# Constants as immediates, a selection matrix from POOL, and one more filter chunk turned by TensorE

## The chip, the cores and the metric

The kernel runs on one core of a Trainium2 chip. A core has five engines with queues of their own: TensorE (PE in the profile; its weight loads are PEld), VectorE (DVE), ScalarE (ACT), GpSimd (POOL) and SyncE (SP), which here issues all transfers. The metric is the device time of one execution in microseconds, as the median of several runs; lower is better.

## The reference

Two independent heads share one output, side by side in the last axis. All inputs are bfloat16, the sequence has S = 2048 rows and the width is D = 576.

```python
def _A_ref(q, k, v, shift_k, ssm_k, ssm_D):     # a gated long convolution
    k_shift = sum over t < 4 of k_pad[:, t:t + S, :] * shift_k[:, 3 - t]
    kv = k_shift * v
    y = irfft(rfft(kv, padded to 2S) * rfft(ssm_k, padded to 2S))[:, :S]
    y = y + kv * ssm_D
    return q * y

def _B_ref(x, wqkv, wo):                        # linear attention, 32 heads of 18
    q, k, v = split(x @ wqkv)
    phi = lambda t: where(t > 0, t + 1, exp(t)) + 1e-6
    num, den = phi(q) @ (phi(k).T @ v), phi(q) @ sum(phi(k))
    return (num / (den + 1e-6)) @ wo
```

## The kernel before

**Order and buffers.** The whole program is one hand-made order of units, the table `ORDER` (L32 to L58): each word names a unit, its chunk and parts, the engine that does its copies (D VectorE, A ScalarE, P POOL) and, after the slash, the buffers it takes. The engines then run their shares strictly in the order in which the table issues them, and semaphores join them. So a unit's place in the table is its place on every engine that it uses, SP's queue included. PSUM is cut into four slots, numbered 0 to 3, of 4 KB per partition (two banks each). A tile may be written into a slot only when the tile that stood there last has been read. In `u1.2.0.0.A/03` the 0 is an SBUF buffer for the result and the 3 the PSUM slot.

**Head A.** The width is cut into five chunks of 128 (the last 64). A chunk's filter row set `h_sb` (128 channels x 2048 taps) must be turned so that taps lie on partitions: `hT`, by the unit hT (L507). Three ways exist. With 'D' TensorE turns 16 pieces of 128 x 128 into one PSUM slot (L516) and VectorE copies the slot out (L311). With 'a' ScalarE first sorts the row by 16 strided runs into `hp` (L521) and a DMA transfer turns it (L525). With 'p' POOL sorts (L523) instead. Chunks 0 to 2 use 'D', chunk 3 'a', chunk 4 'p'. The buffers of `h_sb`, `hp` and `hT` are three, numbered 0 to 2. A unit hd (L501) adds the skip weight `ssm_D` to the first tap.

Then both the turned filter (h) and the product `kv` (u, made by conv on VectorE and POOL) go through a two-stage Fourier transform: `s1` multiplies with the cosine and sine matrices `G` on TensorE into `s_ps` (L537), the result is copied out as `Ch` or `Cu`, a DMA transfer turns it (`Cth`, `Ctu`, unit tr), `s2` does the second stage (L560) and is copied out as `T` or `SU`. `prod` multiplies the two spectra (L572 to L577), `i1` (L594, copied out as `V`) and `i2` (L607 to L609) go back and multiply by `q`. The chunks overlap: while chunk 1 is in its products, chunk 2 is in s1 and chunk 3's filter is turned.

The matrices `G` are made in the kernel, as Sin on ScalarE of an integer phase, with the bias minus pi (L231); a small matrix of 16 points the same way (L236). The bias is a column `negpi` in SBUF, to which the instruction points.

**Head B.** `b_k` and `b_q` multiply x with the weights; `phi` (L446) does exp(t - 1) on ScalarE with the bias column `neg1` (L448) and the rest in one VectorE instruction (L449). There are 16 of these for k, 8 for q and 2 for q's last 64 columns. `b_G` (L655) multiplies x with phi(k) into `g_ps`, 4 full products and one of 64 columns; VectorE copies one column of each to `ex` (L652), and ScalarE adds it as a bias when it copies the rest (L653). The denominators are spread over the 18 columns of a head by matmuls with a selection matrix `esel` (128 x 576): row p has ones in the 18 columns of head p mod 32 (bc and bt, L749 and L760). It is made early by unit es (L105): ScalarE copies four 32 x 32 blocks of the identity and then widens them.

**Around the fourth turn.** The table issues the inverse stage of chunk 0, whose last three units (`i1.0.0.1.A/0`, `i1.0.1.0.A/1`, `i1.0.1.1.A/3`) have ScalarE copy V out, the last of them from PSUM slot 3. Then come products of chunk 1, conv of chunk 2, two s2 copies `SU`, the second transfer of `F` (FT.1.T, `G` turned), hT.3, hd.4, G.3 (slot 1), conv of chunk 3, and `u1.2.0.0.A/03`, which is the first s1 of chunk 2's u and takes slot 3.

Of the kernel before, what the change touches and what calls it, by code (L numbers as in the profile page):

```python
# [9 lines left out]
BF = mybir.dt.bfloat16  # L10
I32 = mybir.dt.int32
I16 = mybir.dt.int16
ACT = mybir.ActivationFunctionType
ALU = mybir.AluOpType
# [6 lines left out]
TWO_PI = 2.0 * math.pi  # L21
# [20 lines left out]
h1.2.1.1.A/1 cv.2.1.DD pT.0.0.P hd.3 pS.0.0.D q.1.1/3 h2.1.0.0.A/32 h2.1.0.1.A/0 G.1/1 cv.2.2.DP h1.2.0.0.A/2 pA.0.1.N  # L42
h1.2.0.1.A/0 u2.1.1.1.D/03 zs/01 ut.1.0/1 u2.1.1.0.A/2 pA.0.0.N i1.0.0.0.D/13 i1.0.0.1.A/0 i1.0.1.0.A/1 zz/2
i1.0.1.1.A/3 pX.1.1.D/0 pA.1.1.N vl.1/0 cv.2.3.DDD ht.2.0/0 pT.1.1.D u2.1.0.1.A/10 u2.1.0.0.A/2 ht.2.1/1 FT.1.T
hT.3.a/02 hd.4 G.3/1 cv.3.0.D cv.3.1.DD u1.2.0.0.A/03 lwv pS.1.1.D u1.2.1.1.A/0 G.0/2 cv.3.2.DD u1.2.1.0.A/1 pX.1.0.D/1
pA.1.0.N u1.2.0.1.A/3 G.4/0 h2.2.1.1.A/22 cv.3.3.DDD h2.2.1.0.A/1 ut.2.0/1 G.2/3 h2.2.0.0.D/00 wom lwo i2.0.1/2
h2.2.0.1.A/1 u2.2.0.0.A/03 i2.0.0/0 h1.3.0.1.D/11 ut.2.1/0 h1.3.0.0.A/2 h1.3.1.0.A/3 kv/0 u2.2.0.1.A/2 h1.3.1.1.A/1
pT.1.0.D pS.1.0.D i1.1.1.1.A/03 hT.4.p/01 i1.1.1.0.A/0 cv.4.0.D den/2 cv.4.1.PP ht.3.1/1 u2.2.1.1.D/11 i1.1.0.1.D/3
i1.1.0.0.A/0 pX.2.0.D/0 u2.2.1.0.A/1 M.2.A/2 i2.1.0/3 i2.1.1/0 M.3.A/1 ht.3.0/0 h2.3.1.1.A/12 bc.2/31 st.0 u1.3.1.1.A/00
u1.3.0.0.A/2 bt/3 h1.4.1.0.A/10 u1.3.0.1.A/1 h2.3.1.0.D/2 pT.2.0.P u1.3.1.0.A/0 h2.3.0.1.A/33 bc.0/12 M.1.A/0 ut.3.0/1  # L50
h1.4.1.1.D/1 h1.4.0.1.A/3 h2.3.0.0.A/0 bc.3/23 pS.2.0.N h1.4.0.0.A/1 M.0.A/0 ut.3.1/0 pA.2.0.P M.4.A/1 bc.1/20
# [53 lines left out]
def _esel(tc, cpool, K):  # L105
    nc = tc.nc
    K.esel = cpool.tile([128, D], BF, name="esel")
    e32 = cpool.tile([128, 32], BF, name="e32")
    for p in range(0, 128, 32):
        nc.scalar.activation(out=e32[p:p + 32, :], in_=K.ident[p:p + 32, p:p + 32], func=ACT.Copy)  # L110
    nc.scalar.activation(out=K.esel[:].rearrange("p (h e) -> p h e", e=18),
                         in_=e32[:].unsqueeze(2).to_broadcast([128, 32, 18]), func=ACT.Copy)


def _small(tc, cpool, slot, K):
# [110 lines left out]
def _sine(tc, cpool, K, ri, h):  # L226
    b = slice(8 * h, 8 * h + 8)
    if ri not in K.G:
        K.G[ri] = cpool.tile([128, 16, 128], BF, name="G%d" % ri)
    src = K.mp[:, b] if ri else K.mc[:, 1, b]  # L230
    tc.nc.scalar.activation(out=K.G[ri][:, b], in_=src, func=ACT.Sin, scale=TWO_PI / 8192, bias=K.negpi[:])  # L231


def _sine16(tc, K):
    nc = tc.nc
    nc.scalar.activation(out=K.sm[:, 1536:1984], in_=K.wi, func=ACT.Sin, scale=TWO_PI / 16, bias=K.negpi[:])  # L236
    nc.scalar.preload_act_table_set("natural_log_exp_and_others")
    nc.scalar.activation(out=K.warm[:], in_=K.neg1[:], func=ACT.Exp)

# [14 lines left out]
def kernel(  # L254
# [13 lines left out]
    nc = tc.nc  # L268
# [18 lines left out]
    cpool = ctx.enter_context(tc.tile_pool(name="consts", bufs=1, side="left"))  # L287
# [68 lines left out]
    K = Consts()  # L356
# [88 lines left out]

    def phi(ps_ap, out_ap, n):  # L446

        nc.scalar.activation(out=out_ap, in_=ps_ap, func=ACT.Exp, bias=K.neg1[0:n, :])  # L448
        nc.vector.scalar_tensor_tensor(out=out_ap, in0=out_ap, scalar=1.0, in1=ps_ap, op0=ALU.min, op1=ALU.max)  # L449

    def b_k(r):
        ps = psum.tile([128, 1024], FP32, name="k_ps")
        rr = r % 4
        for n0, n1 in ((0, 512), (512, 576)):
            for t in range(5):
                nc.tensor.matmul(ps[:, n0:n1], lhsT=xT[r // 4][:, t, rr * 128:(rr + 1) * 128],  # L456
                                 rhs=wqk[:, t, D + n0:D + n1], start=(t == 0), stop=(t == 4))
        phi(ps[:, 0:D], pk[:, r, 0:D], 128)

    def b_q(g, half):  # L460
        ps = psum.tile([128, 2, 512], FP32, name="q_ps")
        for j in range(2):
            c = 2 * half + j
            for t in range(5):
                nc.tensor.matmul(ps[:, j, :], lhsT=wqk[:, t, 128 * c:128 * c + 128], rhs=xT[g][:, t, :],  # L465
                                 start=(t == 0), stop=(t == 4))
        phi(ps[:], pqT[:, 2 * half:2 * half + 2, g * 512:(g + 1) * 512], 128)

    def b_qt(p):
        ps = psum.tile([128, 512], FP32, name="qt_ps")  # L470
        for t in range(5):
            for i, g in enumerate(PAIR[p]):
                nc.tensor.matmul(ps[64 * i:64 * i + 64, :], lhsT=wqk[:, t, 512:576], rhs=xT[g][:, t, :],
                                 start=(t == 0), stop=(t == 4))
        phi(ps[:], pq4[:, p, :], 128)
# [350 lines left out]
    def store_A(i):  # L826
# [8 lines left out]
        'dl': load_D, 'dc': turn_D, 'id': lambda: _ident(tc, cpool, K), 'io': lambda: _small(tc, cpool, slotx, K),  # L835
        'ix': lambda p, h: _dft_index(tc, slotx, K, p, h), 'iv': lambda: _w16_phase(tc, K),
        'iw': lambda: _w16_index(tc, K), 'wk': lambda: _w16_mask(tc, K), 'sin': lambda ri, h: _sine(tc, cpool, K, ri, h),
        'sw': lambda: _sine16(tc, K), 'W': lambda: _w16(tc, cpool, K),
        'FT': f_T, 'hc': lambda: _head_consts(tc, cpool, K), 'es': lambda: _esel(tc, cpool, K), 'xd': x_D,
        'hl': h_load, 'hd': h_D, 'hT': h_T,  # L840
        'kl': lambda g: load_g('k', k, g),
# [53 lines left out]
```

## Time and profile before

| | |
|---|---|
| median of 3 runs | 157.73 us (157.4 to 157.91) |
| span of the profiled execution, first to last instruction | 156.1 us |
| median less span | 1.6 us |
| TensorE clock granted | 1.000 |
| ScalarE sort of chunk 3 (L521) | 4.04 us, from 78.62 |
| DMA queue q1, share of 16 engines' span | 90.7% |
| HBM read, written | 14.97 MB, 4.72 MB |

The page's execution has a span of 156.1 us; it lists no separate time for that execution, so the median of the runs stands beside it. Sums are made against the span and carried to the median with the difference of 1.6 us.

How to read the rows quoted below: a timeline row has start and length in microseconds, the engine, the line, the operation, output<-input with shapes, a count, and in brackets how long the engine stood idle before and what released it. A row of the chain has start, length and what. A row of groups has the count, the busy time, the mean length of one in ns, and the idle time before.

### The profile page before, as it was taken

Reading aid. Unit: us, or ns where it says so; the run is one execution under the profiler, and the core shown is the slowest. Engines: PE = TensorE matmul, PEld = TensorE weight load, DVE = VectorE, ACT = ScalarE, POOL = GpSimd, SP = SyncE. Lnnn points to the kernel's source line nnn. Section 1 sums busy time; section 2 is a strip of 40 time slices with the busy share of each in tenths; the row PEclk is TensorE's granted clock in tenths of the full one; section 3 lists DMA queues with packets and bytes.
Section 4 is the critical chain, followed back from the end, with each engine's and each line's share of the span. In section 5 each row is a group of like instructions: output and inputs, shape, how many; then the busy total and the mean of one; then the engine's idle time right before and its main releaser. Section 6 shows DMA issues by size and latency. Waiting matters only on the chain.

```text
span 156.1 us, 4608 instructions
## 1 busy us (share of the span) xinstructions
PE 148.3 (95%) x1986; PEld 90.6 (58%) x1986; DVE 134.2 (86%) x169; ACT 130.8 (84%) x162; POOL 60.3 (39%) x70
## 2 busy tenths in 40 slices
PE   7999999999999999999999999999988999999990
PEld 2686564466633456457566558767555656568650
DVE  6989769899899798997899999899999979997530
ACT  4999999989998899959999767997998978897431
POOL 6038701908310974007300019457999050230000
PEclk9999999999999999999999999999999999999999
DMA  2997999999999699999999879977779997636086
GB/s 92 380 294 188 296 300 145 252 296 281 201 178 234 135 312 235 166 231 302 178 171 199 220 134 232 144 139 136 231 156 179 149 325 187 156 117 182 0 231 197
DMA packets 74315, 31.92 MB, mean 204 GB/s; under 512 B 52090, under 2 KB 73653, under 8 KB 74294
## 3 DMA queue, kind: packets, MB, share of 16 engines
q1 hardware_dynamic: 74294, 31.62, 90.7%
q8 instruction: 15, 0.25, 0.6%
q14 instruction: 6, 0.05, 0.1%
HBM read 14.97 MB, written 4.72 MB: 126 GB/s over the span
## 4 chain that ended last, share of the span: by engine, by line
PE 62%; DMA 12%; ACT 11%; DVE 8%; issue 2%; POOLq 2%; POOL 1%; SPq 1%; DVEq 0%; ACTq 0%
PE k_ps L456 10%; PE g_ps L662 10%; PE s_ps L537 8%; PE q_ps L465 6%; DMA q<-in_A_q_dram 6%; PE i_ps L594 5%; PE s_ps L560 4%; PE o_ps L783 4%; DMA Cth<-Ch 3%; DMA Ctu<-Cu 3%; DVE q L609 2%; DVE pqT L753 2%; PE i_ps L607 2%; PE i_ps L608 2%; ACT G L231 2%
## 5 line engine op out<-in xcount | busy, mean ns | idle before, releaser
L456 PE MATMUL k_ps<-wqk,xT 128*128 128x512 bf16 (+1 forms) x160 | 21.5, 286 | 0.0
L537 PEld LDWEIGHTS <-G 128*128 128x128 bf16 x320 | 17.2, 98 | 3.1 <-issue 2.3
L465 PE MATMUL q_ps<-xT,wqk 128*128 128x512 bf16 x80 | 18.4, 380 | 0.0
L309 ACT ACTIVATE Cu<-s_ps 128x1024 bf16<-128x1024 f32 (+1 forms) x19 | 17.3, 957 | 0.4 <-PE s_ps L537 0.2
L456 PEld LDWEIGHTS <-xT 128*128 128x128 bf16 x160 | 11.4, 98 | 10.5 <-issue 0.3
L662 PE MATMUL g_ps<-pk,x_sb 128*128 128x512 bf16 (+1 forms) x128 | 16.5, 286 | 0.0
L309 ACT ACTIVATE V<-i_ps 128x1024 bf16<-128x1024 f32 x16 | 15.5, 1025 | 1.1 <-PE i_ps L594 0.8
L309 ACT ACTIVATE Ch<-s_ps 128x1024 bf16<-128x1024 f32 (+1 forms) x17 | 15.7, 952 | 0.3 <-PE s_ps L537 0.3
L309 ACT ACTIVATE T<-s_ps 128x1024 bf16<-128x1024 f32 x15 | 14.8, 1026 | 0.8 <-PE s_ps L560 0.7
L309 ACT ACTIVATE ob<-o_ps 128x576 bf16<-128x576 f32 (+1 forms) x14 | 8.8, 635 | 7.4 <-PE o_ps L775 4.2
L783 PE MATMUL o_ps<-wo_M,pqT 128*128 128x512 bf16 (+1 forms) x112 | 15.0, 287 | 0.0
L495 DVE TENSOR_TENSOR at<-at 128x2048 bf16<-128x2048 bf16 (+1 forms) x12 | 14.2, 1181 | 0.9 <-POOL at L494 0.4
L449 DVE SCALAR_TENSOR_TENSOR pk<-pk,k_ps 128x576 bf16<-128x576 bf16 x16 | 11.9, 752 | 3.4 <-ACT pk L448 3.2
L309 ACT ACTIVATE SU<-s_ps 128x1024 bf16<-128x1024 f32 x14 | 14.1, 1027 | 0.7 <-PE s_ps L560 0.6
L494 DVE TENSOR_TENSOR at<-k,Wj 128x2048 bf16<-128x2048 bf16 (+1 forms) x12 | 14.1, 1171 | 0.0
L495 POOL TENSOR_TENSOR at<-at 128x1024 bf16<-128x1024 bf16 (+1 forms) x3 | 8.3, 2772 | 14.0 <-DVE at L494 10.9
L609 DVE TENSOR_TENSOR q<-i_ps,q 128x1024 bf16<-128x1024 f32 (+1 forms) x10 | 11.0, 1114 | 3.1 <-PE i_ps L608 2.8
L662 PEld LDWEIGHTS <-x_sb 128*128 128x128 bf16 x128 | 8.4, 97 | 8.9 <-issue 1.2
L448 ACT ACTIVATE pk<-k_ps,neg 128x576 bf16<-128x576 f32 x16 | 11.6, 741 | 1.5 <-PE k_ps L456 1.0
L465 PEld LDWEIGHTS <-wqk 128*128 128x128 bf16 x80 | 7.4, 98 | 9.2 <-issue 1.5
L783 PEld LDWEIGHTS <-pqT 128*128 128x128 bf16 x112 | 7.5, 98 | 7.9 <-issue 1.2
L594 PE MATMUL i_ps<-W,T 64*128 64x128 bf16 x160 | 11.2, 217 | 0.6 <-DVE pqT L753 0.5
(163 smaller groups left out, 336.0 us busy)
## 6 DMA issues: line engine op xcount, KB each, us to landing
x_sb<-in_B_x_dram SPq DMA_DIRECT2D x4, 576.0 KB, 6.9
h_sb<-in_A_ssm_k_dram SPq DMA_DIRECT2D x4, 512.0 KB, 5.8
out_dram<-ob SPq DMA_DIRECT2D x7, 288.0 KB, 4.0
k<-in_A_k_dram SPq DMA_DIRECT2D x1, 1280.0 KB
v<-in_A_v_dram SPq DMA_DIRECT2D x1, 1280.0 KB
q<-in_A_q_dram SPq DMA_DIRECT2D x1, 1280.0 KB, 8.6
wqk<-in_B_wqkv_dram SPq DMA_DIRECT2D x2, 576.0 KB, 8.4
k<-in_A_k_dram SPq DMA_DIRECT2D x1, 1024.0 KB, 8.8
```

Source lines behind the costliest of these rows:

```text
L309: nc.scalar.activation(out=out, in_=in_, func=ACT.Copy)
L448: nc.scalar.activation(out=out_ap, in_=ps_ap, func=ACT.Exp, bias=K.neg1[0:n, :])
L449: nc.vector.scalar_tensor_tensor(out=out_ap, in0=out_ap, scalar=1.0, in1=ps_ap, op0=ALU.min, op1=ALU.max)
L456: nc.tensor.matmul(ps[:, n0:n1], lhsT=xT[r // 4][:, t, rr * 128:(rr + 1) * 128], rhs=wqk[:, t, D + n0:D + n1], start=(t == 0), stop=(t == 4))
L465: nc.tensor.matmul(ps[:, j, :], lhsT=wqk[:, t, 128 * c:128 * c + 128], rhs=xT[g][:, t, :], start=(t == 0), stop=(t == 4))
L494: on[0].tensor_tensor(out=t_, in0=kk[:, 3 - stage:19 - stage], in1=wb(stage), op=ALU.mult)
L495: on[1].tensor_tensor(out=a_, in0=a_, in1=t_, op=ALU.add)
L537: nc.tensor.matmul(ps[:, bi, 0:dc], lhsT=K.G[ri][:, b, :], rhs=xf(b), start=True, stop=True)
L594: nc.tensor.matmul(ps[:, r, g, :], lhsT=s[key, hf][64 * r:64 * r + 64, z, x, 128 * g:128 * g + 128], rhs=K.W[64 * r:64 * r + 64, m, :], st ...
L609: nc.vector.tensor_tensor(out=qs, in0=ps[:, :, 0:dc], in1=qs, op=ALU.mult)
L662: nc.tensor.matmul(ps[:, n0:n1], lhsT=x_sb[:, r, f0:f0 + fn], rhs=pk[:, r, n0:n1], start=(r == 0), stop=(r == 15))
L783: nc.tensor.matmul(pss[i][:, n0:n1], lhsT=pqT[:, c, r * 128:(r + 1) * 128], rhs=B['M'][:, c, n0:n1], start=(c == 0 and not first), stop=(c ...
```

## The change

Four edits:

1. The bias of all Sin and of phi's Exp is a number in the instruction, no longer a pointer to a column. The columns are still filled, and two tiny table-warming instructions still use them.
2. `esel` is made by POOL alone: filled with ones, then four selections, each on 32 partitions x 576, keep the ones of the own head.
3. hT.3 goes from 'a' to 'D': TensorE turns it into PSUM slot 3, VectorE copies it to buffer 0. Sort and transfer go.
4. hT.4 keeps 'p', but its sorted copy goes to buffer 2, because buffer 0 now holds chunk 3's turned filter.

```diff
-hT.3.a/02 hd.4 G.3/1 cv.3.0.D cv.3.1.DD u1.2.0.0.A/03 lwv pS.1.1.D u1.2.1.1.A/0 G.0/2 cv.3.2.DD u1.2.1.0.A/1 pX.1.0.D/1
+hT.3.D/03 hd.4 G.3/1 cv.3.0.D cv.3.1.DD u1.2.0.0.A/03 lwv pS.1.1.D u1.2.1.1.A/0 G.0/2 cv.3.2.DD u1.2.1.0.A/1 pX.1.0.D/1
...
-pT.1.0.D pS.1.0.D i1.1.1.1.A/03 hT.4.p/01 i1.1.1.0.A/0 cv.4.0.D den/2 cv.4.1.PP ht.3.1/1 u2.2.1.1.D/11 i1.1.0.1.D/3
+pT.1.0.D pS.1.0.D i1.1.1.1.A/03 hT.4.p/21 i1.1.1.0.A/0 cv.4.0.D den/2 cv.4.1.PP ht.3.1/1 u2.2.1.1.D/11 i1.1.0.1.D/3
...
     K.esel = cpool.tile([128, D], BF, name="esel")
-    e32 = cpool.tile([128, 32], BF, name="e32")
+    nc.gpsimd.memset(K.esel[:], 1.0)
     for p in range(0, 128, 32):
-        nc.scalar.activation(out=e32[p:p + 32, :], in_=K.ident[p:p + 32, p:p + 32], func=ACT.Copy)
-    nc.scalar.activation(out=K.esel[:].rearrange("p (h e) -> p h e", e=18),
-                         in_=e32[:].unsqueeze(2).to_broadcast([128, 32, 18]), func=ACT.Copy)
+        m = K.esel[p:p + 32].rearrange("p (h e) -> p h e", e=18)
+        nc.gpsimd.affine_select(out=m, in_=m, compare_op=ALU.is_equal, fill=0.0, base=0,
+                                pattern=[[-1, 32], [0, 18]], channel_multiplier=1)
...
-    tc.nc.scalar.activation(out=K.G[ri][:, b], in_=src, func=ACT.Sin, scale=TWO_PI / 8192, bias=K.negpi[:])
+    tc.nc.scalar.activation(out=K.G[ri][:, b], in_=src, func=ACT.Sin, scale=TWO_PI / 8192, bias=-math.pi)
...
-    nc.scalar.activation(out=K.sm[:, 1536:1984], in_=K.wi, func=ACT.Sin, scale=TWO_PI / 16, bias=K.negpi[:])
+    nc.scalar.activation(out=K.sm[:, 1536:1984], in_=K.wi, func=ACT.Sin, scale=TWO_PI / 16, bias=-math.pi)
...
-        nc.scalar.activation(out=out_ap, in_=ps_ap, func=ACT.Exp, bias=K.neg1[0:n, :])
+        nc.scalar.activation(out=out_ap, in_=ps_ap, func=ACT.Exp, bias=-1.0)
```

What this moves on the engines, as the difference of the two programs. On ScalarE, at the place of hT.3 (V, SU and wv_GT are the copies named above, Dcol the skip weights):

```order
 L309 ACTIVATE V<-i_ps 128x8x32x4 x3
 L309 ACTIVATE SU<-s_ps 128x2x512 x2
-L521 ACTIVATE hp<-h_sb 128x2048
 L505 ACTIVATE h_sb<-h_sb,Dcol 64x1
 L653 ACTIVATE wv_GT<-g_ps,ex 128x576
```

The sort is gone, and the skip weight of chunk 4 and the copy of G.3 follow the two SU directly.

On VectorE, at the same place (T is a product of spectra of chunk 1, ex the column of G.3, at the conv of chunk 3):

```order
 L498 TENSOR_TENSOR v<-at,v 128x16x128
 L574 TENSOR_TENSOR T<-SU,T 128x2048
+L311 COPY hT<-hT_ps 128x2048
 L652 COPY ex<-g_ps 128x1
 L492 TENSOR_TENSOR at<-k,Wj 128x2048
```

A copy of the turned chunk now stands between the product and the ex column.

On TensorE 16 pairs of a weight load and a turn, of which the first is shown, are put between the s2 stage of chunk 1 and G.3:

```order
 L560 LDWEIGHTS W_329
 L560 MATMUL s_ps<-Ctu,W_329 32x512
+L516 LDWEIGHTS h_sb
+L516 MATMUL hT_ps<-ident,h_sb 128x128
...
 L662 LDWEIGHTS x_sb
 L662 MATMUL g_ps<-pk,x_sb 128x512
```

G.3's matmuls come after the turns; everything later on TensorE keeps its order.

## The prediction

> **What bounds the kernel now.** I read the page's busy shares and its chain first, then a table of stretches, then the timeline around the changed places.
>
> ```profile
> span 156.1 us, 4608 instructions
> PE 148.3 (95%) x1986; PEld 90.6 (58%) x1986; DVE 134.2 (86%) x169; ACT 130.8 (84%) x162; POOL 60.3 (39%) x70
> PE 62%; DMA 12%; ACT 11%; DVE 8%; issue 2%; POOLq 2%; POOL 1%; SPq 1%; DVEq 0%; ACTq 0%
> 30.00:48.20 18.20, 17.80 (x171) 9.86 (x172) 17.08 (x17) 16.99 (x19) 6.11 (x5) 1.00 1.10 240
> 48.20:104.00 55.80, 55.80 (x841) 34.52 (x841) 51.31 (x65) 48.12 (x54) 21.13 (x8) 1.00 1.02 205
> 104.00:120.00 16.00, 14.37 (x210) 8.79 (x207) 15.88 (x15) 14.01 (x20) 14.18 (x6) 1.00 0.80 172
> ```
>
> The last three rows are stretches: length, then the busy time of PE, PEld, DVE, ACT and POOL with their instructions, the granted clock and the load of the DMA engines. Averages mislead here: from 48.2 to 104 us TensorE has no idle time at all, and from 104 to 120 VectorE is the full one (15.88 of 16). A busy TensorE could still be a paced one, so I look at the chain where the new work goes, and at an earlier turn of a filter chunk:
>
> ```profile
> 38.97 0.99 PE hT_ps L516 x16
> 75.75 0.56 PE s_ps L560 x16
> 76.31 4.06 PE g_ps L662 x32
> 80.37 0.91 PE s_ps L537 x16
> 81.27 3.95 PE g_ps L662 x32
> ```
>
> The pieces join without gaps: TensorE issues at its own pace there, and any microsecond put on it is paid. ScalarE is busy, but up to 104 us the page gives little sign that TensorE waits for it.
>
> **Fourth chunk turned by TensorE.** The old ScalarE sort goes, with its transfer; in their place come 16 turns and one VectorE copy.
>
> ```profile
> 74.10 2.85 ACT L309 ACTIVATE V<-i_ps 128x1024 bf16<-128x1024 f32 x3
> 76.24 3.94 PE L662 MATMUL g_ps<-pk,x_sb 128*128 128x512 bf16 x26
> 78.62 4.04 ACT L521 ACTIVATE hp<-h_sb 128x2048 bf16<-128x2048 bf16 x1
> 80.07 1.22 DVE L574 TENSOR_TENSOR T<-SU,T 128x2048 bf16<-128x2048 bf16 x1
> 80.21 1.07 PE L537 MATMUL s_ps<-v,G 128*128 128x128 bf16 x16
> 81.20 0.15 DVE L652 COPY ex<-g_ps 128x1 f32<-128x1 f32 x1
> 82.68 0.74 ACT L653 ACTIVATE wv_GT<-g_ps,ex 128x576 bf16<-128x576 f32 x1
> 85.58 0.74 ACT L653 ACTIVATE wv_GT<-g_ps,ex 128x576 bf16<-128x576 f32 x1 [0.35 <-DVE ex L652]
> 95.66 1.52 PE L537 MATMUL s_ps<-hT,G 128*128 128x128 bf16 x24
> L311 DVE COPY hT<-hT_ps 128x2048 bf16<-128x2048 bf16 x3 | 3.7, 1219 | 0.1
> L516 PE MATMUL hT_ps<-ident,h_sb 128*128 128x128 bf16 x48 | 3.5, 225 | 0.1
> hT<-hp SPq DMA_TRANSPOSE x2, 4.1
> ```
>
> What it removes: ScalarE is free of 4.04 us at 78.6. That is worth nothing by these rows: at 85.58 ScalarE already waits for VectorE, so the sort's delay was used up within 3 us, under the g_ps matmuls. The dropped transfer could start at 78.62 + 4.04 = 82.66 and takes 4.1 to land (last row), so its data lay ready at 86.8 for the matmuls at 95.66: no gain. On SP the loads queued behind it go out earlier, and what they load is read later still: 0, and no row shows a loss from it.
>
> What it adds, step by step, in the time of before. The turns write PSUM slot 3, whose last tile is that of the third V eviction, which ends at 74.10 + 2.85 = 76.95. TensorE is at this point at 76.24, so it now waits 0.71 us. Sixteen turns take 0.99: 77.94. The g_ps product (4.06) ends at 82.00. Next on TensorE stands s_ps<-v,G for u1.2.0.0, again in slot 3, so it must wait for VectorE's copy of the turns. VectorE is in order and full: it finishes T at 81.20 (where the next instruction starts today) and copies until 81.20 + 1.22 = 82.42. So s_ps starts at 82.42 instead of 80.21: **+2.21 us**, of which 0.71 is the wait for V, 0.99 the turns and 0.42 the wait for the copy (the last 0.09: the chain's 4.06 for g_ps is a little longer than the records' 80.21 - 76.24). Behind that matmul all of TensorE's work is queued; behind the copy stand the ex column, for which ScalarE waits at 82.68 (it comes at about 82.5, so no loss), and the conv products. VectorE is 1.22 later after the copy, and the next ex, which ScalarE reads at 85.58, would be ready 1.22 later by that; but the g_ps that it reads is 2.2 later, so VectorE waits too, and both engines run some 2.2 us late from there. In the full TensorE stretch to 104 nothing gives that back.
>
> Bounds: 0.99 if both waits vanish; nothing if the delay ends in idle time later (a rival below); 2.9 if the later copy makes one more slot late by about as much as the V wait (0.71). I take 2.2, since both of its ends come from rows a few microseconds apart.
>
> The Trainium skill, "TensorE: Matmul & The Clock Gate", Part 4 (PE-mode transpose), says that a turn takes about 275 ns in a kernel and does not count towards keeping the clock up. By it, as an estimate, sixteen would take 4.4 us. The row above has 16 in 0.99 us, and every stretch quoted has granted clock 1.00, so by this trace the rule does not hold here.
>
> **Constants in ScalarE's instructions.** 26 exponentials and 5 sines lose a pointer operand.
>
> ```profile
> L448 ACT ACTIVATE pq<-qt_ps,neg 128x512 bf16<-128x512 f32 x2 | 1.4, 687 | 0.0
> L743 ACT ACTIVATE Gz<-den_ps 128x512 bf16<-128x512 f32 x1 | 0.6, 597 | 0.0
> L448 ACT ACTIVATE pk<-k_ps,neg 128x576 bf16<-128x576 f32 x16 | 11.6, 741 | 1.5 <-PE k_ps L456 1.0
> 3.61 1.15 ACT L231 ACTIVATE G<-mp,negpi 128x1024 bf16<-128x1024 int16 x1 [1.31 <-DVE sm L428]
> 8.16 1.16 ACT L231 ACTIVATE G<-mc,negpi 128x1024 bf16<-128x1024 int16 x1
> 9.38 0.62 PE L537 MATMUL s_ps<-hT,G 128*128 128x128 bf16 x8 [0.38 <-ACT G L231]
> 11.09 0.35 SPq L443 DMA_DIRECT2D h_sb<-in_A_ssm_k_dram  x1
> 18.97 8.29 SPq L544 DMA_TRANSPOSE Cth<-Ch  x2
> 29.37 0.63 PE L560 MATMUL s_ps<-Cth,W 64*32 64x512 bf16 x16 [0.29 <-DMA Cth<-Ch]
> 48.20 0.41 PE L560 MATMUL s_ps<-Ctu,W 64*32 64x512 bf16 x8 [0.32 <-DMA Ctu<-Cu]
> ```
>
> Two exponentials of one size, with and without the pointer: 687 and 597 ns, so 90 ns each. The 26 exponentials save 26 x 0.09 = 2.3 us of ScalarE, all before the g_ps products. TensorE does not wait for them: the longest waits that the trace names on it, from the first exponential to 48.2 us, end at transfers (29.37, 48.20), and after that it is full. Nothing, then. The sines are different: three of them stand in a row on ScalarE ahead of the matmul at 9.38, which waits for the third; the turns behind that matmul release the load at 11.09, from which SP's issues run on without pause to the transfers that TensorE waits for. So 3 x 0.09 = **-0.27 us**, carried through. Bounds: 0, if those transfers are paced by the engines that move them and not by their issue; -0.4, if the fourth sine stands on the path too and 0.1 comes off each.
>
> **Selection matrix on POOL.**
>
> ```profile
> L110 ACT ACTIVATE e<-ident 32x32 bf16<-32x32 bf16 x4 | 0.9, 222 | 0.0
> L111 ACT ACTIVATE esel<-e 128x576 bf16<-128x576 bf16 x1 | 0.7, 682 | 0.0
> L87 POOL TENSOR_SCALAR_AFFINE_SELECT maskbd<-maskbd 128x126 bf16<-128x126 bf16 x1 | 0.3, 337 | 0.1
> L96 POOL TENSOR_SCALAR_AFFINE_SELECT hsel<-hsel 64x32 bf16<-64x32 bf16 x2 | 0.4, 208 | 0.0
> 26.85 4.07 POOL L494 TENSOR_TENSOR at<-k,Wj 128x2048 bf16<-128x2048 bf16 x1 [7.65 <-DVE at L495]
> 107.95 0.86 PE L749 MATMUL bc_ps<-Gz,esel 32*128 32x512 bf16 x4
> ```
>
> ScalarE loses 4 x 0.222 + 0.682 = 1.6 us near 22 us. If that time were on the path it would be worth at most the waits of TensorE that end at transfers (0.29 and 0.32 above). But by the program those transfers wait for evictions that stand on ScalarE before it, and their issue at 18.97 comes ahead of it. I count nothing. POOL gains a fill and four selections of 576 elements. From 208 ns at 32 and 337 at 126 elements comes 1.37 ns each, so 0.95 us a selection and, with a fill below 1 us, about 4.8 us. POOL idles 7.65 before 26.85, and the result is read at 107.95: hidden, 0. If a selection took over 1.7 us, the multiplication at 26.85 would slip; at the two rows' lower end (0.34 each) nothing happens either.
>
> The last chunk's sorted copy only moves to another slot, whose last readers are now the turns, done at 78 us, while POOL's copy still waits for the last g_ps product: 0.
>
> **Sum.** 156.1 + 2.2 - 0.3 = 158.0 for the span. The median shown, 157.73, lies 1.6 above this span, which the change does not touch: 159.6.
>
> **Rivals.**
> (1) *The delay ends in idle time.* TensorE idles 1.63 us from 104 to 120 because VectorE is full; if VectorE's 1.22 us of new work fits in its gaps (20.62 busy of 22 from 82 to 104), the lateness of TensorE is swallowed there. For it speaks the third window row; against it, that VectorE's gaps are waits for the same late TensorE.
>
> ```profile
> 82.00:104.00 22.00, 22.00 (x390) 14.78 (x388) 20.62 (x32) 18.06 (x22) 8.10 (x4) 1.00 0.88 183
> ```
>
> It would give 157.4 (the gain in front alone) to 158.1 (with 0.7 us left over).
> (2) *ScalarE paces the stretch up to the g_ps products after all, and it comes out faster.* If the evictions that free PSUM set TensorE's rhythm, up to 2.3 + 1.6 + 0.3 = 4.2 us come back before the new work costs 2.2: 157.7 + 2.2 - 4.2 = 155.7 at best. It decides from 2.7 us of gain on, more than half of what is freed. For it: ACT has 11% of the chain and is 16.99 of 18.2 busy from 30 to 48.2. Against it: 0.4 us of idle PE is all there is in that stretch, and the chain's pieces run at bare matmul pace.
> (3) *The turns run slowly*, one after the other's end: 16 x 0.225 without overlap is 3.6 us instead of 1.0, so 162.2. The row at 38.97 speaks against it. (The Trainium skill's 275 ns a turn, cited above, points this way.)
> (4) *The pointers stay.* If an immediate costs what a pointer does, the -0.27 is gone: 159.9.
>
> **How the numbers follow.** Forecast 0.66 (158.3 to 160.6), rival 1 0.15, rival 2 0.15, rivals 3 and 4 0.02 each. A measurement of this kernel tells some 0.3% (0.5 us) from no change. Slower: 0.66 + 0.02 + 0.02 = 0.70; same 0.15; faster 0.15. The top, 160.6, is the bound of 2.9 with no gain in front; below, the range takes in rival 1 and the weaker part of rival 2, down to 157.2, and leaves out about 0.12 below and 0.05 above.
>
> **What would show it.** Right: TensorE idle for about 0.7 us ahead of the hT_ps turns near 76.5 with ACT V as its releaser, and about 0.4 ahead of s_ps<-v,G with the hT copy on VectorE as releaser; ACT almost idle from 79 to 82; pk exponentials near 650 ns; POOL's selections below 1.7 us; the wait at 29.37 about 0.3 earlier. Wrong: if the pieces after 82 stand where they stood, or if the wait at 48.20 has moved forward by more than 0.5 us.

## The result, and the profile after

| | before | after |
|---|---|---|
| median of 18 runs each | 159.13 us (157.31 to 502.0) | 160.04 us (159.57 to 162.88) |
| span of the profiled execution | 156.1 us | 158.6 us |
| ratio of the times, after to before | | 1.014 (1.0111 to 1.017) |

Some runs of both kernels fell into a slower state, which brings the medians to within 0.91 us of each other, so the ratio, which leaves these runs out, is the measure: 1.4% slower, about 2.2 us on 157.73. The forecast, 159.6 against 157.73, was a ratio of 1.012, which lies inside the interval. First the page of the changed kernel: span, busy shares, the chain of waits by engine, the main DMA queue.

```profile
span 158.6 us, 4616 instructions
PE 148.6 (94%) x1984; PEld 91.3 (58%) x2002; DVE 135.4 (85%) x170; ACT 123.4 (78%) x156; POOL 66.2 (42%) x75
PE 72%; DVE 12%; DMA 9%; ACT 3%; issue 1%; SPq 0%; DVEq 0%
q1 hardware_dynamic: 72214, 31.10, 88.6%
```

ScalarE is busy 7.4 us less than before (130.8), POOL 5.9 more, and the kernel is slower: neither was the bound. ACT falls from 11% of the chain to 3%, and PE rises from 62% to 72%. Now three stretches of the changed kernel, laid out as in the prediction.

```profile
48.20:75.50 27.30, 27.14 (x389) 16.14 (x392) 24.61 (x28) 23.18 (x29) 13.01 (x4) 1.00 1.12 229
75.50:82.50 7.00, 5.90 (x69) 3.59 (x68) 6.93 (x8) 3.41 (x6) 0.00 (x0) 1.00 1.09 179
106.30:122.30 16.00, 14.39 (x216) 8.87 (x209) 15.88 (x15) 13.93 (x19) 14.19 (x6) 1.00 0.80 169
```

TensorE, full from 48.2 to 104 before, now has a hole of 1.1 us in the 7 us from 75.5. The last row is the one that could have swallowed the delay: 14.39 busy of 16, before 14.37. Nothing was swallowed. The timeline of the same place:

```profile
73.82 2.86 ACT L309 ACTIVATE V<-i_ps 128x1024 bf16<-128x1024 f32 x3
75.40 0.63 PE L560 MATMUL s_ps<-Ctu,W 64*32 64x512 bf16 x16
76.73 1.16 PE L516 MATMUL hT_ps<-ident,h_sb 128*128 128x128 bf16 x16 [0.70 <-ACT V L309]
80.92 1.22 DVE L311 COPY hT<-hT_ps 128x2048 bf16<-128x2048 bf16 x1
82.19 1.05 PE L537 MATMUL s_ps<-v,G 128*128 128x128 bf16 x16 [0.34 <-DVE hT L311]
82.24 0.74 ACT L653 ACTIVATE wv_GT<-g_ps,ex 128x576 bf16<-128x576 f32 x1 [3.59 <-DVE ex L652]
```

Both forecast waits are there with the forecast releasers: 0.70 for V (forecast 0.71) and 0.34 for the copy (0.42). ScalarE, freed of the sort, waits for 3.59 us there (last row), as announced. From the s2 matmul ahead of the place to s_ps<-v,G it is 82.19 - 75.40 = 6.79 us. Before it was 80.21 - 75.68 = 4.53. The first of these rows of the kernel before has that start; the others are of later places where the two kernels differ:

```profile
75.68 0.62 PE L560 MATMUL s_ps<-Ctu,W 64*32 64x512 bf16 x16
113.73 4.64 SPq L544 DMA_TRANSPOSE Ctu<-Cu  x2
118.53 0.63 PE L560 MATMUL s_ps<-Ctu,W 64*32 64x512 bf16 x16
152.58 0.41 ACT ob L309
```

The same places in the changed kernel (timeline, and the last row of its chain):

```profile
115.70 5.43 SPq L544 DMA_TRANSPOSE Ctu<-Cu  x2
120.71 0.63 PE L560 MATMUL s_ps<-Ctu,W 64*32 64x512 bf16 x16 [0.20 <-DMA Ctu<-Cu]
154.72 0.41 ACT ob L309
```

A new wait of 0.20 us for a transfer stands at 120.71, and the issue ahead of it takes 5.43 instead of 4.64. So the profiled execution can be cut into four parts: the **front** (to the s2 matmul near 75), the **place** (from there to s_ps<-v,G), the **rest** (from there to the last ob copy), the **tail** (from there to the end of the span).

| | front | place | rest | tail | span |
|---|---|---|---|---|---|
| before | 75.68 | 4.53 | 72.37 | 3.52 | 156.1 |
| after | 75.40 | 6.79 | 72.53 | 3.88 | 158.6 |
| difference | -0.28 | +2.26 | +0.16 | +0.36 | +2.50 |
| forecast | -0.27 | +2.21 | 0 | 0 | +1.94 |

In these two profiles the forecast's two terms are met, and two small ones that it did not have make up the difference. The single edits, from the groups of the changed kernel and its timeline:

```profile
L448 ACT ACTIVATE pk<-k_ps 128x576 bf16<-128x576 f32 x16 | 10.3, 652 | 2.6 <-PE k_ps L456 2.1
L448 ACT ACTIVATE pq<-qt_ps 128x512 bf16<-128x512 f32 x2 | 1.2, 597 | 0.1
L516 PE MATMUL hT_ps<-ident,h_sb 128*128 128x128 bf16 x64 | 4.7, 227 | 0.7 <-ACT V L309 0.7
L111 POOL TENSOR_SCALAR_AFFINE_SELECT esel<-esel 32x576 bf16<-32x576 bf16 x4 | 3.5, 886 | 0.2
8.00 1.07 ACT L231 ACTIVATE G<-mc 128x1024 bf16<-128x1024 int16 x1
11.02 0.35 SPq L443 DMA_DIRECT2D h_sb<-in_A_ssm_k_dram  x1
26.33 4.08 POOL L494 TENSOR_TENSOR at<-k,Wj 128x2048 bf16<-128x2048 bf16 x1 [1.19 <-DVE at L495]
29.54 0.63 PE L560 MATMUL s_ps<-Cth,W 64*32 64x512 bf16 x16 [0.59 <-DMA Cth<-Ch]
47.92 0.41 PE L560 MATMUL s_ps<-Ctu,W 64*32 64x512 bf16 x8
```

An exponential is 89 to 90 ns shorter (741 to 652, 687 to 597), a turn no slower (227 against 225 ns), a selection takes 0.89 us (estimate 0.95). POOL's slack before its multiplication shrank from 7.65 to 1.19 us, more than the new work of 4.3 us explains. The third sine ends at 9.07 instead of 9.32, so the three save their 0.25; but the load that follows on SP starts at 11.02 instead of 11.09, and the wait at 29.37 is not 0.3 earlier, as was announced, but 0.17 later and longer (0.59). The matmul that stood at 48.20 is 0.28 earlier.

### The profile page after: what moved, and what is told of

Same layout as the page of the kernel before. It is cut to its first block, busy times and chain, and to the rows that moved or that the text cites. A ratio compares the mean times of both kernels' runs of the same rounds, so it can differ in the third digit from the quotient of the medians.

```text
span 158.6 us, 4616 instructions
## 1 busy us (share of the span) xinstructions
PE 148.6 (94%) x1984; PEld 91.3 (58%) x2002; DVE 135.4 (85%) x170; ACT 123.4 (78%) x156; POOL 66.2 (42%) x75
## 4 chain that ended last, share of the span: by engine, by line
PE 72%; DVE 12%; DMA 9%; ACT 3%; issue 1%; SPq 0%; DVEq 0%
DMA Cth<-Ch 9%; PE k_ps L456 9%; PE o_ps L783 9%; PE s_ps L537 8%; PE g_ps L662 8%; PE q_ps L465 7%; PE i_ps L594 7%; PE s_ps L560 5%; DVE pqT L753 5%; PE i_ps L607 3%; PE warm_ps L79 3%; PE i_ps L608 2%; PE o_ps L775 2%; DVE hT L311 2%; DVE q L609 1%; PE hT_ps L516 1%
## 5 line engine op out<-in xcount | busy, mean ns | idle before, releaser
L662 PE MATMUL g_ps<-pk,x_sb 128*128 128x65 bf16 (+1 forms) x124 | 16.1, 283 | 0.2
L783 PE MATMUL o_ps<-wo_M,pqT 128*128 128x64 bf16 (+1 forms) x106 | 14.1, 281 | 0.6 <-issue 0.5
L448 ACT ACTIVATE pk<-k_ps 128x576 bf16<-128x576 f32 x16 | 10.3, 652 | 2.6 <-PE k_ps L456 2.1
L653 ACT ACTIVATE wv_GT<-g_ps,ex 128x576 bf16<-128x576 f32 x5 | 3.7, 741 | 10.7 <-DVE ex L652 10.7
```

Of the source, the lines that this page charges most:

```text
L662: nc.tensor.matmul(ps[:, n0:n1], lhsT=x_sb[:, r, f0:f0 + fn], rhs=pk[:, r, n0:n1], start=(r == 0), stop=(r == 15))
L783: nc.tensor.matmul(pss[i][:, n0:n1], lhsT=pqT[:, c, r * 128:(r + 1) * 128], rhs=B['M'][:, c, n0:n1], start=(c == 0 and not first), stop=(c ...
```

## Experiments

Each kernel's ratio is to the kernel before, measured beside it on the same chip. One table first, of the four parts, made for each profiled execution from the starts of the same rows as above (three profiles, with spans of 158.0, 161.0 and 364.3 us, are not in it):

| kernel | front | place | rest | tail |
|---|---|---|---|---|
| turn alone | 76.52 | 6.78 | 72.55 | 3.45 |
| other PSUM slots | 75.02 | 6.79 | 72.53 | 3.86 |
| copy by ScalarE | 74.79 | 6.29 | 72.54 | 3.38 |
| slots, copy by ScalarE | 75.35 | 5.56 | 72.54 | 3.45 |
| constants | 74.79 | 4.54 | 72.32 | 3.45 |
| sines only | 75.33 | 4.54 | 72.32 | 3.51 |
| exponentials only | 75.17 | 4.54 | 72.33 | 3.46 |
| matrix | 74.82 | 4.53 | 72.32 | 3.53 |
| constants and matrix | 75.08 | 4.52 | 72.33 | 3.47 |
| after, again | 75.38 | 6.79 | 72.52 | 3.81 |
| after, one transfer more | 74.69 | 6.79 | 72.31 | 3.21 |
| after, one ScalarE copy more | 74.73 | 6.80 | 72.53 | 3.44 |
| after, both more | 74.86 | 6.80 | 72.31 | 3.53 |

Among kernels with the same edit there, the place and the rest repeat within 0.05 us, so a single profile tells them. The front does not: the changed kernel, its repetition and the kernels that differ from it only behind 75 us lie from 74.69 to 75.40. What the front is worth must come from ratios of many runs.

### The turn: which wait sets its price

Theory: the turn costs 2.2 us, by two waits that lie one behind the other. Rivals: the V wait alone, the turns alone, or ScalarE's rhythm. First the kernel before with the turn only (edits 3 and 4).

```diff
-hT.3.a/02 ... hT.4.p/01
+hT.3.D/03 ... hT.4.p/21
```

> Before with the fourth chunk turned by TensorE alone (hT.3 by TensorE and VectorE, hT.4's sorted copy in buffer 2); constants and selection matrix as before. Forecast's theory: all the loss is here, 2.2 us over the kernel before (ratio 1.014); s_ps<-v,G of u1.2.0.0 starts 2.2 us later than in before, behind the copy of hT. Rival (a part of the loss comes from the constants or from POOL's selections): clearly less than 2.2 us here, 1.5 or less.

Ratio 1.0108 (1.0048 to 1.0168). By the ratio alone the rival's 1.5 us is possible, but the place takes 6.78, which is 2.25 more than before, so the turn carries the loss. The timeline has both waits:

```profile
77.85 1.15 PE L516 MATMUL hT_ps<-ident,h_sb 128*128 128x128 bf16 x16 [0.70 <-ACT V L309]
83.30 0.89 PE L537 MATMUL s_ps<-v,G 128*128 128x128 bf16 x13 [0.35 <-DVE hT L311]
```

Next, the changed kernel with other PSUM slots, so that V is not in the way:

```diff
-hT.3.D/03 hd.4 G.3/1 ... u1.2.0.0.A/03 ... u1.2.1.0.A/1 ... u1.2.0.1.A/3
+hT.3.D/01 hd.4 G.3/3 ... u1.2.0.0.A/01 ... u1.2.1.0.A/3 ... u1.2.0.1.A/1
```

> The changed kernel with PSUM slots renamed: the turns in slot 1, G.3 in slot 3, u1.2.0.0 in 1, u1.2.1.0 in 3, u1.2.0.1 in 1. The turns no longer wait for the third V eviction. Forecast's theory: the two waits lie one behind the other on TensorE but the end is set by VectorE's copy alone, so u1.2.0.0 starts where it did and nothing is gained: 2.0 us over before, as the changed kernel, the wait for the copy growing from 0.34 to 1.0 us. Rival (the waits add): 0.7 us are gained, 1.3 us over before.

Ratio 1.0155 (1.0069 to 1.0241).

```profile
75.58 1.23 PE L516 MATMUL hT_ps<-ident,h_sb 128*128 128x128 bf16 x16
81.81 1.05 PE L537 MATMUL s_ps<-v,G 128*128 128x128 bf16 x16 [1.06 <-DVE hT L311]
```

The wait for V is gone and TensorE starts the turns sooner (0.56 behind the s2 matmul instead of 1.33), but the wait for the copy grows from 0.34 to 1.06, and the place takes 6.79 as before the edit. VectorE's copy sets the end; the wait for V only stood ahead of it. So the copy goes to ScalarE, which idles there:

```diff
-hT.3.D/03
+hT.3.A/03
```

> The changed kernel with the turned chunk copied out by ScalarE instead of VectorE, slots as in the changed kernel. ScalarE is idle there and would copy at about 78.5 to 80.4, ahead of the end of G.3. Forecast's theory: the wait for the copy goes, the wait for V (0.7) and the turns (1.0) stay: 1.7 less 0.3 in front, so 1.4 us over before. Rival (VectorE's 1.2 us set the loss, all later work being paced by it): the whole loss but the turns is gone, about 0.7 us over before. Rival (ScalarE paces): 2.0 or more over before.

Ratio 1.0081 (1.0035 to 1.0127). Then both together:

```diff
-hT.3.D/03 hd.4 G.3/1 ... u1.2.0.0.A/03 ... u1.2.1.0.A/1 ... u1.2.0.1.A/3
+hT.3.A/01 hd.4 G.3/3 ... u1.2.0.0.A/01 ... u1.2.1.0.A/3 ... u1.2.0.1.A/1
```

> The slots of the run e4_slots and the copy by ScalarE of the run e5_actcopy together. Forecast's theory: no wait is left, only 16 turns of TensorE's time: 1.0 less 0.3 in front, so 0.7 us over before. Rival (the turns cost no time of their own, since TensorE's lateness is taken up in its idle time from 104 us on): equal to before or 0.3 us under it.

Ratio 1.005 (1.0006 to 1.0094). The first two rows are of the copy by ScalarE alone, the last two of both edits:

```profile
76.12 1.17 PE L516 MATMUL hT_ps<-ident,h_sb 128*128 128x128 bf16 x16 [0.70 <-ACT V L309]
81.08 1.06 PE L537 MATMUL s_ps<-v,G 128*128 128x128 bf16 x16
...
75.91 1.21 PE L516 MATMUL hT_ps<-ident,h_sb 128*128 128x128 bf16 x16
80.91 1.06 PE L537 MATMUL s_ps<-v,G 128*128 128x128 bf16 x16
```

With ScalarE's copy the second wait goes (place 6.29), and now the slots are worth their 0.73: 5.56, which is 1.03 above the kernel before, the bare turns. The price of the turn is thus put together as forecast, and it can be halved. Even so the turn never gains: nothing waited for the sort that it replaces.

### The constants and the selection matrix

Theory: the sines give 0.27 us, the exponentials and the matrix nothing. Rival: ScalarE paces the first 48 us. The constants alone (edit 1):

```diff
-... func=ACT.Sin, scale=..., bias=K.negpi[:])
+... func=ACT.Sin, scale=..., bias=-math.pi)
-... func=ACT.Exp, bias=K.neg1[0:n, :])
+... func=ACT.Exp, bias=-1.0)
```

> Before with the constants as immediates alone (5 sines, 26 exponentials). Forecast's theory: 0.27 us under before, from three sines in a row; the exponentials (2.3 us of ScalarE) give nothing. Rival (ScalarE paces up to the g_ps products): 1.5 to 2.6 us under before. Rival (the front is paced by the warm-up matmuls, VectorE's copy of hT and the transfers): 0.0.

Ratio 0.9976 (0.9942 to 1.0011). Only the sines:

```diff
-... func=ACT.Sin, scale=..., bias=K.negpi[:])
+... func=ACT.Sin, scale=..., bias=-math.pi)
```

> Before with the immediates in the 5 sines only. Forecast's theory: the same 0.27 us under before as with all constants. Rival (exponentials matter): clearly less gain than the run e1_consts. Rival (front paced by others): 0.0.

Ratio 0.9989 (0.9956 to 1.0022). Only the exponentials:

```diff
-... func=ACT.Exp, bias=K.neg1[0:n, :])
+... func=ACT.Exp, bias=-1.0)
```

> Kernel before with the constant in the 26 exponentials only, the sines as before. Theory (TensorE waits for no exponential that the sum needs): ratio 0.999 to 1.001, although ScalarE saves 26 x 0.09 = 2.3 us. Rival (the exponentials of the first 30 us delay the copies Ch that the transfers wait for): ratio 0.997 to 0.998, and the second-stage matmul that stood at 29.37 starts 0.3 earlier.

Ratio 0.9986 (0.9947 to 1.0026). None differs from 1 by its interval. The 2.3 us that the exponentials save are not seen in the time; a gain of up to some 0.8 us is not excluded. With the sines alone the load on SP starts at 10.89 instead of 11.09, so 0.20 of the 0.27 arrive there. The matrix alone (edit 2):

```diff
-        nc.scalar.activation(out=e32[p:p + 32, :], ...)
-    nc.scalar.activation(out=K.esel[:]..., in_=e32[:]..., func=ACT.Copy)
+    nc.gpsimd.memset(K.esel[:], 1.0)
+        nc.gpsimd.affine_select(out=m, in_=m, ...)
```

> Before with the selection matrix made by POOL alone. Forecast's theory: no difference, 0.0 us; the four selections are near 0.95 us each and end before POOL's first multiplication at 26.9. Rival (the chain's step by ScalarE ahead of a transfer is real): up to 0.6 us under before. Rival (POOL's first multiplication slips): slower by the slip.

Ratio 0.9966 (0.9932 to 1.0), where no change was expected. ScalarE's copies Ch are indeed earlier with it; the first row is of this kernel, the second of the one before:

```profile
21.67 1.93 ACT L309 ACTIVATE Ch<-s_ps 128x1024 bf16<-128x1024 f32 x2
...
23.21 1.92 ACT L309 ACTIVATE Ch<-s_ps 128x1024 bf16<-128x1024 f32 x2
```

To see whether these 1.5 us are the gain, POOL makes the matrix and ScalarE does about its old work too, the result of which nothing uses (the diff is against the kernel with the matrix alone):

```diff
+        nc.scalar.activation(out=e32[p:p + 32, :], ...)
+    for _ in range(2):
+        nc.scalar.activation(out=edum..., in_=e32[:]..., func=ACT.Copy)
     nc.gpsimd.memset(K.esel[:], 1.0)
```

> Selection matrix made on POOL as in the change, but ScalarE does about its old work as well: the four block copies and, into a tile that nothing reads, two widenings of 256 columns, in all some 1.6 us. Theory S (the gain of the matrix edit, 0.9966, is ScalarE's freed time ahead of the copies Ch): the gain is gone, ratio 0.999 to 1.001, and the Ch copies stand near 23.2 us again instead of 21.7. Rival P (the gain comes from POOL's other timing or is spread between executions): ratio 0.996 to 0.998 although ScalarE is as late as before.

Ratio 0.9954 (0.9913 to 0.9995). ScalarE is as late as before in it; both rows are of this kernel, whose profile lies some 2.8 us later here as a whole:

```profile
22.19 0.74 ACT L455 ACTIVATE pk<-k_ps,neg 128x576 bf16<-128x576 f32 x1 [0.18 <-PE k_ps L463]
26.23 1.92 ACT L316 ACTIVATE Ch<-s_ps 128x1024 bf16<-128x1024 f32 x2
```

From this exponential to the copies it is 4.04 us, in the kernel before 3.85 (19.36 to 23.21), with the matrix alone 2.31 (19.36 to 21.67). The ratio stays below 1 all the same, so a gain by ScalarE's freed time is not borne out. Whether the ratio shows POOL's timing or only the scatter of the front stays open: the fastest run with the matrix alone (156.87) is no faster than the fastest one of the kernel before beside it (156.84). Last, the constants and the matrix together (the diffs of both edits above), measured twice:

> Before with constants and selection matrix of the change, without the fourth chunk's turn: the version that should beat both. Forecast's theory: 0.3 us under before (ratio 0.998). Rival (ScalarE paces): 2 us under. Rival (front paced by others): 0.0.

> Kernel before with the constants in the instructions and the selection matrix on POOL, chunk 3 still sorted by ScalarE (the pair of edits measured once already, at a ratio of 0.9952). Theory F (both edits act on the front, ahead of the wait near 48.2 us, and add up): ratio 0.994 to 0.997, span 155.0 to 155.5, the s2 matmul on Ctu that stood at 48.20 now at 47.2 to 47.9, and the last ob copy as far behind it as before. Rival N (the front is only the spread between executions): ratio 0.998 to 1.002.

Ratios 0.9952 (0.9908 to 0.9997) and 0.9916 (0.9874 to 0.9959). By these ratios this version, the change without its turn, is faster than both kernels: by 0.5 to 0.8% against the one before, and by more against the changed one. The size is less sure than the sign: the fastest runs differ by 0.27 us (156.57 against 156.84) and 0.34 us (156.68 against 157.02), the ratios by 0.75 and 1.3 us. In the second profile theory F's signs are there: the s2 matmul stands at 47.59, and the last ob copy 104.34 us behind it, 104.38 before. The changed kernel was run beside the second of these:

> The changed kernel again, beside the pair above on the same chip, so that the turn alone is their difference. Theory A (all parts add): 2.2 to 2.5 us above the pair, ratio to the kernel before about 1.010 to 1.011. Rival B (the front's gain is lost once the turn is there, because the later work waits for transfers whose time the front does not set): 2.8 us or more above the pair, ratio 1.013 to 1.015.

Ratio 1.0161 (1.0088 to 1.0233). The spans are 155.4 and 158.5, so 3.1 us apart, above the 2.2 to 2.5 of theory A and as rival B has it. By the table 2.27 of it lie at the place, 0.19 in the rest, 0.34 in the tail and 0.30 in front. Rival B's mechanism, a lost gain of the front, could thus be worth 0.30 at most in these two profiles, and that is within the front's scatter; it is neither shown nor excluded.

### The two terms without a step: an instruction load that moved

The rest is 72.5 in every kernel with the turn and 72.3 to 72.4 without. The tail is 3.8 to 3.9 in the changed kernel, its repetition and the one with other slots, and 3.4 to 3.5 in all others up to here. The DMA queues show a difference at both places: q14 carries loads of instructions, six in each kernel. In the changed kernel one lies at 119.6 us instead of 108.7, and the last at 156.4 instead of 139.0. The first three rows are of the kernel before, two from 113.7 to 118.5 us (the last Ctu transfers) and one from 153 us to the end; the rows behind the dots are of the changed kernel, from 115.7 to 120.7 and from 155.5 to the end (packets, MB, share of 16 engines).

```profile
q1 hardware_dynamic: 2774, 0.70, 79.7%
q8 instruction: 1, 0.02, 1.3%
q1 hardware_dynamic: 661, 0.54, 51.3%
...
q1 hardware_dynamic: 2821, 0.73, 88.6%
q14 instruction: 1, 0.01, 0.4%
...
q1 hardware_dynamic: 537, 0.40, 38.6%
q14 instruction: 1, 0.01, 1.0%
```

The kernel before thus has an instruction load among these transfers too, of another queue, q8, and no wait; that some load falls there is not enough. With a q14 load there, the issue of the two transfers on SP takes 5.35 to 5.47 us in every profile of the table, without one 4.5 to 5.0. That speaks for SP being held up; which engine q14 serves, no view names.

The idea to be tested is that an engine that executes fewer instructions comes to its next load later, and the change takes one transfer from SP and instructions from ScalarE. So the changed kernel gets one instruction back: a transfer of 32 bytes on SP, at the place of hT.3, or one small copy by ScalarE near 23 us. Nothing reads either.

```diff
+    K.spd = cpool.tile([1, 16], BF, name="spd")
...
+            if ci == 3:
+                nc.sync.dma_start(out=K.spd, in_=A_ssm_D...[:, 0:16])
```

> The changed kernel with one more transfer of 32 bytes on SP at the place of hT.3, where the kernel before had the transposing one; it loads something that nothing reads. In the changed kernel an instruction load (queue q14) falls at 119.6 us instead of 108.5, next to a new wait of TensorE of 0.20 for Ctu at 120.71. Theory Q (with one transfer fewer, SP reaches its instruction load later, among the Ctu transfers, and that is the 0.2): the load returns to about 111, the wait before the Ctu matmul goes, and the time from the first s_ps<-v,G of chunk 2 to the last ob copy is 72.3 instead of 72.5. Rival R (the 0.2 comes with the turn, whatever SP does): the wait stays and the stretch is 72.5.

Ratio 1.0083 (1.003 to 1.0136). The timeline, and the queue from 115 to 119.8 us, where q14 no longer has a line:

```profile
114.99 4.54 SPq L547 DMA_TRANSPOSE Ctu<-Cu  x2
119.80 0.63 PE L563 MATMUL s_ps<-Ctu,W 64*32 64x512 bf16 x16
...
q1 hardware_dynamic: 3016, 0.78, 85.3%
```

The load has moved to 112.6, the issue of the Ctu transfers takes 4.54 instead of 5.43, TensorE no longer waits, and the rest is 72.31.

```diff
+    e32 = cpool.tile([128, 32], BF, name="e32")
+    nc.scalar.activation(out=e32[0:32, :], in_=K.ident[0:32, 0:32], func=ACT.Copy)
     nc.gpsimd.memset(K.esel[:], 1.0)
```

> The changed kernel with one more copy of 32 x 32 by ScalarE near 23 us, where it waits for TensorE; nothing reads it. In the changed kernel the last instruction load falls at 156.4 us, behind all work, and the span ends 3.88 us after the last ob copy starts; in kernels with one ScalarE instruction more it falls near 139 to 143 and the tail is 3.4 to 3.5. Theory Q (the count of ScalarE's instructions sets when that load comes, and at the end it delays the end): the load is at 140 to 143 and the tail 3.4 to 3.5, 0.4 us less. Rival R (the tail is chance, or has another cause): tail 3.8 to 3.9 as in the changed kernel.

Ratio 1.0105 (1.002 to 1.0191). The first wait stays, the last load lies at 140.5 and the tail is 3.44 (queue from 154.4 us to the end, without q14):

```profile
120.06 0.62 PE L562 MATMUL s_ps<-Ctu,W 64*32 64x512 bf16 x16 [0.20 <-DMA Ctu<-Cu]
q1 hardware_dynamic: 688, 0.56, 53.6%
```

With both additions (the two diffs above), and then the changed kernel, without an edit, as their neighbour:

> The changed kernel with both additions of the two runs before it. Theory Q: both late instruction loads gone, span 0.6 us below the changed kernel on the same chip (about 157.8 to 158.1 after the same front), ratio to the kernel before about 1.010. Rival R: as the changed kernel, about 1.014.

Ratio 1.0104 (1.0002 to 1.0206): both terms are gone (72.31 and 3.53), and the place keeps 6.80.

> The changed kernel again, as the neighbour of the three runs before it. Both theories: instruction loads at 119.5 and 156.3, wait for Ctu 0.2, stretch 72.5, tail 3.8 to 3.9, ratio 1.013 to 1.016.

Ratio 1.0109 (1.0023 to 1.0195), below the expected 1.013 to 1.016, which its interval still holds. The neighbour's loads lie at 122.1 and 158.9 of a span of 161.0, and it waits 0.19 for Ctu. The intervals of the four overlap, so the times alone settle nothing here; the rows do. For the rest the cause is shown as far as an added transfer, and nothing else that was tried, takes away load and wait together, twice. The tail is less clean: the added transfer also removed it (last load at 139.1, tail 3.21), with ScalarE's count unchanged, so it is not shown that the load is ScalarE's, as the expectation had it. All four profiles with a q14 load in the last 3 us have the long tail (the neighbour's too: 161.0 - 157.19 = 3.8), and none of the others has.

## Why the prediction was right, and where it was not

The forecast ratio of 1.012 lies inside the measured 1.0111 to 1.017, and the mechanism that makes up most of the sum held. What failed are a step that was put at nothing, the way from the sum to the median, and the path by which the gain in front was to arrive.

- **The sum at the turned chunk** (+2.21) was right: 2.26, and 6.78 to 6.80 for the place in all kernels with VectorE's copy. Its parts are right too: V 0.70, turns about 1.0, copy 0.34. The copy's end on VectorE, not the V wait, sets the sum, since removing the V wait alone changed nothing (6.79).
- **TensorE pays and nothing is given back.** The delay reaches the end: in the stretch with idle time TensorE is busy 14.39 of 16 us, 14.37 before, and the rest is no shorter. Rival 1 falls.
- **Dropped transfer: "0, and no row shows a loss from it".** This step failed. With one transfer fewer a q14 instruction load stands among the Ctu transfers, with a new wait of 0.20 us and a rest 0.16 longer; one added transfer takes both away. For the instructions that go from ScalarE the prediction has no such term either; the last q14 load now stands behind all work, with a tail 0.36 longer, and what links these two is not shown. Together some 0.5 us, most of the distance from the forecast's +1.94 to the span's +2.50.
- **From the span to the median** the prediction added 1.6 us, on the median of three runs, 157.73. Over 18 runs the same kernel has 159.13, so the medians lie 0.91 us apart where 1.87 was forecast; the ratio, 2.2 us, does not have this fault.
- **The gain in front** (-0.27, "carried through"). In the two profiles it is -0.28, but by luck, since the front scatters by 0.7. The sines save 0.25 up to the third one's end, as summed, but of that 0.07 is left at the load on SP in the changed kernel (0.20 with the sines alone), and the announced sign, a wait at 29.37 some 0.3 earlier, did not come. Constants and matrix together give 0.75 to 1.3 us by the ratios and 0.27 to 0.34 by the fastest runs, so their size is open; the matrix, costed at 0, showed 0.9966. ScalarE's freed time is not borne out as the cause there; what is, stays open.
- **Rival 2, ScalarE paces,** falls: it needs 2.7 us of gain, and constants and matrix together give at most 2.0 by their intervals (0.9874), the exponentials alone at most 0.84. **Rival 3** falls: 16 turns in 1.16 us, clock 1.00. The 227 ns of one turn overlap with the next, so adding up single turns was wrong; that a row of turns keeps the clock up, 1 us of them can't tell, and there the prediction's "does not hold here" says too much. **Rival 4** falls: 90 ns are gone from each instruction, although the time does not show it.
- **POOL's cover held, barely.** The selections cost what was estimated, but of 7.65 us of slack 1.19 was left, because other work grew as well (below). With the matrix alone none was left: POOL's multiplication follows its own earlier work without a wait (last row of the document).

## What to carry to other kernels

Where two waits stand one behind the other on a full engine, find the later releaser and price that one: removing the first alone gave 0, removing the second 0.5, both 1.23 us. Moving work to a full TensorE is paid in full, even when the work that it replaces looks costly, if nothing waited for that. And an edit that removes instructions also moves the loads of later ones; compare the place of the instruction loads, by queue, in both traces before putting a few tenths down to the edit's own work.

## What the runs showed of the hardware that was not expected

**Instruction loads have a place, and it matters.** Six loads on q14 of 0.05 MB in all; one among the Ctu transfers went with 0.2 us of wait, one at the very end with 0.35 us of tail. The Trainium skill, "Runtime: NRT & Kernel Launch", section "Instruction fetch mechanics", says that crossing a block costs one queue update, mostly hidden. For the loads elsewhere these runs show nothing against it, the q8 load among the Ctu transfers before the change included. The q14 load there is not hidden: load and wait went together when a transfer was added. For the one at the end only the coincidence is shown.

**POOL's small selections take over five times as long beside VectorE.** In the kernel with the matrix alone, the selections of another small matrix, hsel, come later and meet VectorE's products of two inputs:

```profile
22.35 0.20 POOL L96 TENSOR_SCALAR_AFFINE_SELECT hsel<-hsel 64x32 bf16<-64x32 bf16 x1
22.63 1.13 POOL L98 TENSOR_SCALAR_AFFINE_SELECT hsel<-hsel 64x32 bf16<-64x32 bf16 x1
24.98 1.19 POOL L98 TENSOR_SCALAR_AFFINE_SELECT hsel<-hsel 64x32 bf16<-64x32 bf16 x1
22.47 1.22 DVE L492 TENSOR_TENSOR at<-k,Wj 128x2048 bf16<-128x2048 bf16 x1
24.87 1.23 DVE L495 TENSOR_TENSOR at<-at 128x2048 bf16<-128x2048 bf16 x1
26.53 4.07 POOL L494 TENSOR_TENSOR at<-k,Wj 128x2048 bf16<-128x2048 bf16 x1
```

A selection of this size takes 0.20 us at 22.35 and 1.13 at 22.63; the long ones shown end 0.07 us after a VectorE product does (23.76 and 23.69, 26.17 and 26.10). The Trainium skill, "SBUF — State Buffer", section "SBUF: two separate sides", says that VectorE and GpSimd share a pair of ports, and that where VectorE's instruction has two inputs in SBUF and GpSimd's reads SBUF, the one that starts first has the pair for its whole length; the rows agree. So POOL's slack has to be counted with VectorE's work beside it.
